# Another order of expert visits, and of weight widening beside it, in a fused attention, expert and feed-forward kernel

## The chip, the core and the metric

The kernel runs on one core of one Trainium2 chip. The metric is the device time of one launch in microseconds (us), the median of several executions; lower is better. Besides TensorE (PE), which multiplies matrices, the core has VectorE (DVE), ScalarE (ACT), GpSimd (POOL) and SyncE (SP). SP only issues transfers here. Every engine takes its instructions strictly in the order in which they were written, so an instruction that waits holds up all behind it on its engine.

## What is computed

Three stages follow each other: attention with rotary embedding over 4 batches, 8 heads and 576 positions (2304 tokens of width 512); a mixture of 8 experts, of which each token takes the best one; and a dense feed-forward with an ELU. Cut to what matters here:

```python
logits = xn @ en.T / tau
expert_idx = np.argmax(logits, axis=1)
for e in range(8):
    mask = expert_idx == e
    if not mask.any(): continue
    h = np.maximum(x[mask] @ w1[e], 0.0)               # w1[e]: 512 x 1024
    out[mask] = gate_w[mask, None] * (h @ w2[e])       # w2[e]: 1024 x 512
...
g = ELU(out @ w_in)                                    # w_in, w_out are float64
return g @ w_out
```

Which tokens go where is data. On the inputs of `setup_inputs()`, the reference sends 6, 709, 173, 0, 3, 691, 722 and 0 tokens to the experts 0 to 7. After the first three of the four batches it is 6, 706, 173, 0, 3, 118, 722 and 0.

## The kernel before, in words

Attention is worked pair of heads by pair of heads. As each batch ends, its tokens are routed: DVE counts how many tokens each expert has (`tot`), and GpSimd writes each token's row into the region of its expert in DRAM (`xreg`). Then the experts are worked in **visits** of 128 rows. One visit gathers 128 rows of one expert (`x_gather`, GpSimd), transposes them by a transfer (`x_turn`, SP), multiplies by w1 (`mm1`, four chunks of 24 matmuls, L1050 to L1052), applies `relu` (ACT, then DVE L1063), multiplies by w2 (`mm2`, 24 matmuls, L1087 to L1089), scales (`y_out`, ACT L1099 and DVE L1100) and writes 128 rows to `yreg` (`y_put`). TensorE runs mm1 of visit j+1 ahead of mm2 of visit j.

There are NE early visits, whose experts are chosen by `tab_early` from the counts after three batches (full tiles of 128 rows only, largest expert first), and NL late ones, whose experts are chosen by `tab_head` and `tab_visits` when all batches are counted. Before, NE is 6 and NL 19, so NV = 25 visits are written out. The last seven of them run only if they are needed (`used`), and what is not needed costs one tiny matmul each for mm1 and mm2. On the given inputs 22 are needed. `tab_head` ranks the experts by their visits still to do and then permutes the ranks by the table `pi` = 0, 7, 6, 5, 4, 3, 2, 1: the largest first, then from the smallest up. On the given inputs this order of visits follows, by the code's arithmetic:

- visits 0 to 4 expert 1, visit 5 expert 6 (early); visits 6 to 11 expert 5, 12 expert 4, 13 expert 1, 14 expert 0, 15 and 16 expert 2, 17 to 21 expert 6.

So the weights are loaded for the first visit and changed at visits 5, 6, 12, 13, 14, 15 and 17. A visit whose expert is that of the visit ahead skips loading and conversion by a branch on a register (`chg`, in `when`). A change costs, for one expert, eight loads of 512 KB on SP (`w_load(j, q)`, two each for q = 0 to 3, L1003 for w1 and L1006 for w2) and the split of each float32 chunk into two float16 halves (`w_conv(j, q)`: ACT L1023, then DVE L1025) into one set of buffers `w16`, so that a chunk is converted only when mm1 or mm2 of the visit ahead has used the old one.

Beside the visits, the float64 weights of the feed-forward are **widened**: 32 chunks of 512 KB, 0 to 15 of w_in and 16 to 31 of w_out, each with one `widen_load` (SP, L935 or L939) and five steps of `widen` (ACT L954, DVE L956 to L959, ACT L962 and for w_out four additions L965 to L968 on DVE or GpSimd, ACT L975, GpSimd L977). Chunks 11, 30 and 31 are widened much earlier and parked in DRAM.

**The order of all this is written out by due times.** Every task is put on a list by `add(t, f, ...)` or `addv(a, f, ...)`, the list is sorted by time, and the instructions of all engines are written in that order. In the expert part the unit (`ZU`) is half a visit: mm1 of visit j is due at 2j and mm2 at 2j + 3. `w_conv(j, q)` is due just after the visit ahead has used the chunks of q: at 2j - 1.74 and 2j - 1.24 for q = 0 and 1, at 2j + 1.26 and 2j + 1.76 for q = 2 and 3. `w_load(j, q)` is due as soon as one of 11 pairs of staging buffers is free, and the lists `wc` and `until` take a pair away for good when a widened chunk needs its room. Chunk c is widened at `WT[c]`, its load comes about 3 units earlier or when one of its few buffers is free, and the feed-forward begins at unit 50. There, g = 0 to 8 are groups of 256 rows gathered from `yreg` (`z_gather`, GpSimd; `z_turn`, SP), with `ff1`, `elu`, `ff2`, `fold` and `store`. The first two gathers are due at 37.7 and their transposes at 39.3.

Of the kernel before, what the change touches and what calls it, by code (L numbers as in the profile page):

```python
# [26 lines left out]
ROW = 520  # L27
NE = 6
NL = 19
NV = NE + NL  # L30
OFF = {'MX': 0.8, 'pool': (3, 8), 'pool13': (), 'pool14': (), 'pool15': (), 'rope0': (0, 1, 2, 4, 5), 'rope1': (0, 2), 'hi@1': -1.2, 'lo@1': -2.0, 'stack@1': -2.0, 'conv0': (5,), 'r_base': -0.39, 'r_norm': -0.46, 'r_slot@2': 0.6, 'r_gate': -0.41, 'r_put@0': 2.88, 'r_turn_pe@1': -3.85, 'r_sq@0': -0.13, 'r_rank@1': 0.52, 'r_rank': 0.35, 'r_turn:4': 0.24, 'relu@0': 2.65, 'r_acc_t@3': -0.16, 'r_pow@0': 1.01, 'r_sq@2': 0.29, 'r_base@2': -3.0, 'w_load@0': -0.15, 'x_turn@1': 1.47, 'r_put@1': 0.78, 'r_put:2': 0.5, 'w_load@1': -0.11, 'hi@2': -0.19, 'r_base@0': -0.49, 'r_pow@1': 0.4, 'r_slot:2': 0.04, 'rope2': (4,), 'r_gate@1': -0.33, 'r_gate@3': 0.36, 'r_slot@0': 2.38, 'x_gather@0': 0.7, 'hi': 0.06, 'r_norm@1': 0.22, 'r_acc_t@1': 0.35, 'v_load': 0.99, 'r_turn:0': 1.39, 'v_load@1:2': -0.43, 'r_pick': -0.18, 'r_rank@0': 0.21, 'r_turn': 1.14, 'r_pick@0': -0.28, 'WS': (14, 1.1, 32, 1.3), 'WO': (0, 0.476, 1.351, 1.395), 'WL': 3.126, 'WT': 8.011, 'relu': 0.901, 'y_out': -0.193, 'w_conv': 0.0, 'x_turn': 0.103, 'y_put': 0.0, 'G0': 51.007, 'ZG': -0.28, 'r_lo@1': 0.54, 'r_norm@0:0': -3.95, 'r_norm:0': -0.85, 'r_slot:4': -0.29, 'd_prep@3': -0.21, 'r_acc@13': 0.21, 'r_pick@1': -0.21, 'EO': (0, 0.3, 0.5, 0.7, 1.2), 'ES': (0, 1, 2, 3, 4, 5, 6, 7), 'WH': 0.32, 'WJ': 0.3, 'WE': 0.9, 'FO': (0.2, 0.25), 'E0': (1, 5, 6), 'EC': (0, 1, 2, 3, 4, 6, 7), 'WQ': (0, 1, 2, 3, 4, 8, 12, 14, 15), 'WR': (0, 1, 2, 3, 4, 5, 6, 7, 8, 9, 10, 11, 12, 13, 14, 15, 16, 17, 18, 19, 20, 21, 22, 23, 24, 25, 26, 27, 28, 29, 30, 31), 'c1': (1, 0), 'c2': (1, 0)}
# [13 lines left out]
def kernel(ctx: ExitStack, tc: tile.TileContext, qk, vp, cs, cf, tid, emb, tau, w1, w2, wi, wo, out, tag=None):  # L45
# [6 lines left out]
    yreg = dram.tile([NV * 128, ROW], I32, name="yreg")  # L52
# [578 lines left out]
    def tab_early():  # L631
# [42 lines left out]
        yield  # L674
        nc.vector.tensor_scalar(px, px, float(NE), None, op0=ALU.min)
# [5 lines left out]
        nc.vector.tensor_copy(sidx[:, 0:NE], cpos[:, 0:NE])  # L681
        yield

    def tab_head():
# [13 lines left out]
        nc.vector.scalar_tensor_tensor(key, nvi[:, 0], 8.0, e8, op0=ALU.mult, op1=ALU.subtract)  # L698
# [9 lines left out]
        nc.vector.tensor_tensor(m, rk.unsqueeze(2).to_broadcast([128, 8, 8]), e8.unsqueeze(1).to_broadcast([128, 8, 8]), op=ALU.is_equal)  # L708
        yield
        nc.vector.tensor_tensor(m, m, pi.unsqueeze(1).to_broadcast([128, 8, 8]), op=ALU.mult)  # L710
        yield
        nc.vector.tensor_reduce(out=rk, in_=m, op=ALU.add, axis=AX.X)
# [88 lines left out]
    for p in range(NP):  # L801
# [51 lines left out]
        if p % 4 == 3:  # L853
# [249 lines left out]
    def y_put(j):  # L1103
        nc.gpsimd.dma_start(out=yview[j][128 * j:128 * j + 128, :], in_=x2r.pop(j))
# [270 lines left out]
```

## Time and profile before

| | before |
|---|---|
| median of 3 executions | 1020.54 us (1019.59 to 1024.45) |
| the profiled execution: time, span of its instructions | 1029.22 us, 1027.4 us |
| PE busy | 902.9 us (88%), clock granted 0.95 |
| DVE busy | 694.3 us (68%) |
| ACT busy | 515.8 us (50%) |
| POOL busy | 560.8 us (55%) |
| read from memory | 87.54 MB |

The time is that of the launch, and the span goes from the first to the last instruction. Busy shares are averages over three stages with different limits: attention lasts to about 375 us, the visits from there to about 641, and the feed-forward from 645 to the end. A row of a timeline gives the start, the duration, engine, line, operation and, in brackets, how long the engine sat idle before it and what ended that.

### The profile page before, as it was taken

Reading aid. Unit: us, or ns where it says so; the run is one execution under the profiler, and the core shown is the slowest. Engines: PE = TensorE matmul, PEld = TensorE weight load, DVE = VectorE, ACT = ScalarE, POOL = GpSimd, SP = SyncE. Lnnn points to the kernel's source line nnn. Section 1 sums busy time; section 2 is a strip of 40 time slices with the busy share of each in tenths; the row PEclk is TensorE's granted clock in tenths of the full one; section 3 lists DMA queues with packets and bytes.
Section 4 is the critical chain, followed back from the end, with each engine's and each line's share of the span. In section 5 each row is a group of like instructions: output and inputs, shape, how many; then the busy total and the mean of one; then the engine's idle time right before and its main releaser. Section 6 shows DMA issues by size and latency. Waiting matters only on the chain. (4 is left out here: it accounts for less than half of the span.)

```text
span 1027.4 us, 24659 instructions
## 1 busy us (share of the span) xinstructions
PE 902.9 (88%) x9398; PEld 658.1 (64%) x9398; DVE 694.3 (68%) x1085; ACT 515.8 (50%) x874; POOL 560.8 (55%) x652
## 2 busy tenths in 40 slices
PE   3399998998889779999788995899899999999994
PEld 0144555545455467777555771688788888888884
DVE  8557668777866537888896766685665664665651
ACT  1244564464454624765675543565555554554540
POOL 6465765765634123434772165446776766766640
PEclk8589999999999889999999998899899999999998
DMA  7554565584364566998999873401201201201000
GB/s 257 158 154 113 153 163 129 170 173 115 122 147 165 167 183 142 317 229 228 277 320 284 237 181 90 119 14 42 62 22 43 59 25 43 58 27 42 22 22 20
DMA packets 133494, 136.04 MB, mean 132 GB/s; under 512 B 71528, under 2 KB 109416, under 8 KB 133360
## 3 DMA queue, kind: packets, MB, share of 16 engines
q1 hardware_dynamic: 124400, 106.07, 39.6%
q0 software_dynamic: 8352, 27.62, 8.2%
q8 instruction: 76, 1.25, 0.5%
q10 hardware_dynamic: 608, 0.63, 0.2%
q14 instruction: 58, 0.48, 0.2%
HBM read 87.54 MB, written 17.35 MB: 102 GB/s over the span
## 5 line engine op out<-in xcount | busy, mean ns | idle before, releaser
L1132 PE MATMUL banks<-arena 128*128 128x256 f16 x576 | 158.2, 275 | 2.8 <-ACT arena L1147 2.8
L1134 PE MATMUL banks<-arena 128*128 128x256 f16 x576 | 158.2, 275 | 0.0
L1133 PE MATMUL banks<-arena 128*128 128x256 f16 x576 | 158.2, 275 | 0.0
L364 ACT ACTIVATE arena<-banks 128x576 f32<-128x576 f32 x144 | 90.3, 652 | 124.2 <-PE banks L363 100.5
L1184 PE MATMUL banks<-arena 128*128 128x256 f16 x504 | 138.7, 275 | 5.5 <-DVE arena L1199 5.5
L1167 DVE TENSOR_TENSOR arena<-arena 128x896 f16<-128x896 f32 x72 | 80.2, 1114 | 87.1 <-ACT arena L1163 85.3
L1185 PE MATMUL banks<-arena 128*128 128x256 f16 x504 | 138.7, 275 | 0.0
L1186 PE MATMUL banks<-arena 128*128 128x256 f16 x504 | 138.7, 275 | 0.0
L1050 PE MATMUL banks<-arena 128*128 128x128 f16 x704 | 125.6, 224 | 7.2 <-ACT arena L1023 6.3
L1052 PE MATMUL banks<-arena 128*128 128x128 f16 x704 | 125.4, 225 | 4.7 <-DVE arena L1025 4.4
L1163 ACT ACTIVATE arena<-arena 128x896 f16<-128x896 f32 x71 | 67.5, 951 | 118.6 <-POOL arena L1160 117.3
L1051 PE MATMUL banks<-arena 128*128 128x128 f16 x704 | 125.5, 224 | 0.0
L336 DVE TENSOR_REDUCE MH<-banks 128x1 f16<-128x576 f32 x144 | 103.2, 751 | 31.6 <-PE banks L326 29.9
L1157 POOL TENSOR_TENSOR arena<-arena 128x256 f32<-128x256 f32 x67 | 53.1, 793 | 92.0 <-DVE arena L1154 90.5
L400 PE MATMUL banks<-arena 128*64 128x256 f32 (+9 forms) x768 | 90.2, 360 | 5.2 <-DVE arena L376 3.7
L1025 DVE SCALAR_TENSOR_TENSOR arena<-arena 128x1024 f16<-128x1024 f32 x64 | 82.3, 1324 | 17.2 <-ACT arena L1023 16.5
L977 POOL TENSOR_TENSOR arena<-arena 128x896 f16<-128x896 f32 (+1 forms) x32 | 52.6, 1645 | 69.4 <-ACT arena L975 50.3
L362 PE MATMUL banks<-arena 128*128 128x288 f16 (+1 forms) x320 | 79.6, 299 | 3.3 <-DVE l L522 2.0
L363 PE MATMUL banks<-arena 128*128 128x288 f16 (+1 forms) x320 | 78.7, 295 | 1.0 <-issue 1.0
L326 PE MATMUL banks<-arena 64*128 64x288 f16 (+1 forms) x320 | 47.6, 307 | 35.5 <-DVE MH L336 16.4
L1050 PEld LDWEIGHTS <-arena 128*128 128x128 f16 x704 | 70.9, 101 | 9.5 <-ACT arena L1023 6.9
L1087 PE MATMUL banks<-arena 128*128 128x512 f16 x176 | 67.5, 383 | 10.6 <-ACTq L987 10.1
(237 smaller groups left out, 2284.4 us busy)
## 6 DMA issues: line engine op xcount, KB each, us to landing
arena<-in_w_dram SPq DMA_DIRECT2D x64, 512.0 KB
arena<-in_qk_dram SPq DMA_DIRECT2D x30, 576.0 KB
arena<-in_wo_dram SPq DMA_DIRECT2D x32, 256.0 KB
arena<-in_wi_dram SPq DMA_DIRECT2D x16, 512.0 KB
arena<-arena SPq DMA_DIRECT2D x32, 216.0 KB
yreg<-arena POOLq DMA_DIRECT2D x25, 260.0 KB, 4.2
arena<-arena SPq DMA_DIRECT2D x32, 144.0 KB
arena<-in_vp_dram SPq DMA_DIRECT2D x16, 256.0 KB
```

What stands on the lines that cost most here:

```text
L336: nc.vector.tensor_reduce(out=MH1[p % 2][:, c:c + 1], in_=t[:, :, 0:288], op=ALU.max, axis=AX.XY, negate=True)
L364: nc.scalar.activation(P32[:, (9 * p + i) % RP].rearrange("p (c n) -> p c n", c=2), t[:, :, 0:288], AF.Exp, scale=2.0)
L400: nc.tensor.matmul(o[64 * e:64 * e + 64, c, 0:QC[c].stop - QC[c].start], lhsT=w, rhs=x[:, QC[c]], start=first and n == 0, stop=end and n = ...
L1050: nc.tensor.matmul(o[:, fc], lhsT=w[:, 0, a], rhs=x[:, k], start=k == 0, stop=False)
L1051: nc.tensor.matmul(o[:, fc], lhsT=w[:, 0, a], rhs=x[:, 4 + k], start=False, stop=False)
L1052: nc.tensor.matmul(o[:, fc], lhsT=w[:, 1, a], rhs=x[:, k], start=False, stop=k == 3)
L1132: nc.tensor.matmul(o[:, v], lhsT=wih[k][:, f0:f0 + 128], rhs=z[:, :, k], start=k == 0, stop=False)
L1133: nc.tensor.matmul(o[:, v], lhsT=wih[k][:, f0:f0 + 128], rhs=z[:, :, 4 + k], start=False, stop=False)
L1134: nc.tensor.matmul(o[:, v], lhsT=wil[k][:, f0:f0 + 128], rhs=z[:, :, k], start=False, stop=k == 3)
L1184: nc.tensor.matmul(y, lhsT=a, rhs=b, start=u + f + n == 0, stop=False)
L1185: nc.tensor.matmul(y, lhsT=a, rhs=w[:, 1, WB[i - 1]], start=False, stop=False)
L1186: nc.tensor.matmul(y, lhsT=q[:, 1, f, GB[i - 1]], rhs=b, start=False, stop=u + f == 4 and n == len(m) - 1)
```

## The change

Three things change. **The early visits** are five instead of six, and late ones 20 instead of 19. `yreg` gets `Y0` = 18432 unused rows in front, and the indices into it are raised by as much. **The order of the late visits**: the key by which `tab_head` ranks is raised by 512 for the expert of the last early visit, which so comes first, and the table `pi` gives way to arithmetic that subtracts 3.5 from the ranks 4 to 7: the order is rank 0, 4, 1, 5, 2, 6, 3, 7. On the given inputs, by the code's arithmetic:

- visits 0 to 4 expert 1 (early); visit 5 expert 1, 6 expert 0, 7 to 12 expert 5, 13 expert 4, 14 to 19 expert 6, 20 and 21 expert 2.

The weights are then changed at visits 6, 7, 13, 14 and 20, and 22 visits are needed as before. **The times** of the widening (`WT`), the first due time of loads for late visits (5.4 instead of 8.01) and of gathers (6 instead of 6.9, and no special time for visit 5) are other ones.

```diff
-NE = 6
-NL = 19
+NE = 5
+NL = 20
 NV = NE + NL
+Y0 = E * NTOK
...
-    yreg = dram.tile([NV * 128, ROW], I32, name="yreg")
+    yreg = dram.tile([Y0 + NV * 128, ROW], I32, name="yreg")
...
         nc.vector.tensor_copy(rrl, rr[:, 0, NE - 1:NE])
         yield
+        nc.vector.tensor_scalar(elast, e8, rrl, -512.0, op0=ALU.is_equal, op1=ALU.mult)
+        yield
+        nc.vector.tensor_tensor(elast, elast, e8, op=ALU.add)
+        yield
...
-        nc.vector.scalar_tensor_tensor(key, nvi[:, 0], 8.0, e8, op0=ALU.mult, op1=ALU.subtract)
+        nc.vector.scalar_tensor_tensor(key, nvi[:, 0], 8.0, elast, op0=ALU.mult, op1=ALU.subtract)
...
-        nc.vector.tensor_tensor(m, rk.unsqueeze(2).to_broadcast([128, 8, 8]), e8.unsqueeze(1).to_broadcast([128, 8, 8]), op=ALU.is_equal)
-        yield
-        nc.vector.tensor_tensor(m, m, pi.unsqueeze(1).to_broadcast([128, 8, 8]), op=ALU.mult)
-        yield
-        nc.vector.tensor_reduce(out=rk, in_=m, op=ALU.add, axis=AX.X)
+
+        ps_ = tbv(832, 8)
+        nc.vector.tensor_scalar(ps_, rk, 4.0, -3.5, op0=ALU.is_ge, op1=ALU.mult)
+        yield
+        nc.vector.tensor_tensor(rk, rk, ps_, op=ALU.add)
...
     def x_gather(j):
+        after('tab_early' if j < NE else 'tab_visits')
...
     def y_put(j):
-        nc.gpsimd.dma_start(out=yview[j][128 * j:128 * j + 128, :], in_=x2r.pop(j))
+        nc.gpsimd.dma_start(out=yview[j][Y0 + 128 * j:Y0 + 128 * j + 128, :], in_=x2r.pop(j))
...
-    WT = dict(zip((0, 1, 2, 3, 4, 5, 6, 7, 8, 9, 10, 12, 13, 14, 15), (4.6, 6, 6.65, 7.3, 8.6, 12.5, 14, 14.9, 15.7, 16.4, 17.1, 17.8, 18.5, 19.2, 19.9)))
-    WT |= dict(zip(range(16, 30), (20.8, 21.7, 22.9, 24.2, 25.2, 33.3, 35.3, 37.8, 38.6, 39.4, 40.2, 41, 41.8, 42.6)))
+    WT = dict(zip((0, 1, 2, 3, 4, 5, 6, 7, 8, 9, 10, 12, 13, 14, 15), (4.6, 6, 6.7, 7.4, 8.2, 9, 16, 16.85, 17.7, 18.55, 19.4, 20.25, 21.1, 21.95, 22.8)))
+    WT |= dict(zip(range(16, 30), (23.6, 30, 30.9, 31.8, 32.7, 33.6, 34.5, 35.4, 36.3, 37.2, 38, 39.3, 40.2, 42.2)))
...
-        if j < 6:
-            add(zg0 + 3.4 + .9 * j if j < 5 else max(zg4 + .1, ZV + ZU * 4.3 + .1), x_gather, j)
-        else:
-            addv(max(a - 5.2, 6.9), x_gather, j)
+        if j < NE:
+            add(zg0 + 3.4 + .9 * j, x_gather, j)
+        else:
+            addv(max(a - 5.2, 6), x_gather, j)
...
-        t0 = max(t0, free[b], {0: -4.8, 1: 0}.get(j, 1 if j < 6 else OFF.get('WT', 7.7))) + .001
+        t0 = max(t0, free[b], {0: -4.8, 1: 0}.get(j, 1 if j < NE else 5.4)) + .001
```

Left out are the three shifts of scratch room in `tab_visits` and `tab_compact`, the addition of `Y0` to `sidx` within instructions that were there, and the counts of `steps`, which follow the number of small operations: 24 instead of 22 in `tab_early`, 21 instead of 22 in `tab_head`.

## Rows read from the trace of the kernel before

**Rows 1.** Windows: us; then PE, PEld, DVE, ACT, POOL busy; granted clock; DMA share; GB/s

```profile
375.00:492.20 117.20, 117.20 (x1323) 85.94 (x1321) 97.59 (x164) 64.96 (x101) 48.69 (x62) 0.99 0.86 228
492.20:641.00 148.80, 120.34 (x1228) 83.53 (x1227) 112.55 (x145) 81.75 (x109) 76.70 (x83) 0.93 0.85 236
...
645.00:731.00 86.00, 79.56 (x671) 67.86 (x671) 59.85 (x91) 48.09 (x84) 49.61 (x73) 0.93 0.22 58
731.00:994.00 263.00, 262.55 (x2406) 235.08 (x2403) 157.97 (x211) 139.66 (x235) 175.26 (x255) 1.00 0.15 38
```

**Rows 2.** Timeline of PE: starts of mm1(2) and mm1(11), then around mm2(21)

```profile
386.70 0.22 PE L1050 MATMUL banks<-arena 128*128 128x128 f16 x1
...
481.56 0.22 PE L1050 MATMUL banks<-arena 128*128 128x128 f16 x1
...
622.51 0.60 PE L1076 MATMUL banks<-c,cft 1*128 1x512 f16 x2
633.24 0.58 PE L1087 MATMUL banks<-arena 128*128 128x512 f16 x1 [10.14 <-ACTq L987]
...
640.92 0.82 PE L1076 MATMUL banks<-c,cft 1*128 1x512 f16 x3
```

**Rows 3.** Who waited for whom, PE, 492 to 641 us: us, times, longest

```profile
PE banks L1087 <- ACTq L987: 10.1, 1, 10.1
PE banks L1050 <- ACT arena L1023: 6.3, 2, 3.2
PE banks L1052 <- DVE arena L1025: 4.4, 6, 1.7
PE banks L1088 <- DVE arena L1025: 4.1, 3, 2.2
```

**Rows 4.** Line L1003, w1's loads: durations ns, first and last start; L1006 likewise

```profile
L1003 SPq DMA_DIRECT2D arena<-in_w_dram x32: 72/390/1823, 324.9 to 558.9; - x32
```

**Rows 5.** Window: the stretch in which the transfers moved most

```profile
500.00:525.00 25.00, 18.02 (x143) 12.11 (x142) 22.38 (x23) 19.68 (x25) 18.89 (x20) 0.86 1.07 343
```

**Rows 6.** Groups by line, DVE, 375 to 660 us: count | busy us, mean ns | idle before

```profile
L1025 DVE SCALAR_TENSOR_TENSOR arena<-arena 128x1024 f16<-128x1024 f32 x56 | 72.0, 1324 | 12.6 <-ACT arena L1023 11.9 <-SPq L987 0.3 <-PE banks L1089 0.2
L1063 DVE SCALAR_TENSOR_TENSOR arena<-banks,arena 128x512 f16<-128x512 f32 x50 | 34.2, 685 | 17.2 <-ACT arena L1062 8.4 <-ACTq L987 4.1 <-DVEq L987 2.3
L958 DVE SCALAR_TENSOR_TENSOR arena<-arena 128x512 uint32<-128x512 uint32 x29 | 26.0, 897 | 4.8 <-POOL arena L977 2.3
L959 DVE SCALAR_TENSOR_TENSOR arena<-arena 128x512 uint32<-128x512 uint32 x29 | 23.3, 804 | 1.0
L956 DVE TENSOR_SCALAR arena<-arena 128x512 f32<-128x512 f32 x29 | 18.6, 643 | 5.4 <-DVEq L987 3.4
L1100 DVE SCALAR_TENSOR_TENSOR arena<-banks,arena 128x512 f16<-128x512 f32 x25 | 18.6, 746 | 14.6 <-ACT arena L1099 9.2 <-DVEq L987 3.6 <-ACTq L987 1.7
L957 DVE TENSOR_SCALAR arena<-arena 128x512 uint32<-128x512 uint32 x29 | 15.8, 546 | 1.0
```

**Rows 7.** Timeline of SP: loads of w1 for visit 17; load of chunk 28

```profile
555.66 5.05 SPq L1003 DMA_DIRECT2D arena<-in_w_dram  x4
...
618.27 1.46 SPq L939 DMA_DIRECT2D arena<-in_wo_dram  x2
```

**Rows 8.** Timeline of ACT: first conversion for visit 17; widening of chunk 28

```profile
563.33 1.06 ACT L1023 ACTIVATE arena<-arena 128x1024 f16<-128x1024 f32 x1 [5.34 <-DMA arena<-in_w_dram]
...
624.29 0.66 ACT L954 ACTIVATE arena<-arena 128x512 f32<-128x512 f32 x1 [5.39 <-DMA arena<-in_wo_dram]
```

**Rows 9.** What SP itself waited for, 370 to 660 us: us, times, longest

```profile
SPq L935 <- DVE arena L959: 26.3, 5, 20.7
```

**Rows 10.** Timeline of DVE, 611 to 615 us: two first steps of widening chunk 27

```profile
611.83 0.42 DVE L956 TENSOR_SCALAR arena<-arena 128x512 f32<-128x512 f32 x1
612.28 2.00 DVE L957 TENSOR_SCALAR arena<-arena 128x512 uint32<-128x512 uint32 x1
```

**Rows 11.** Timeline of POOL in the same stretch

```profile
612.01 2.00 POOL L977 TENSOR_TENSOR arena<-arena 128x896 f16<-128x896 f32 x1 [0.77 <-ACT arena L975]
```

More of the change, by code (lines that the diff above doesn't have):

```diff
@@ L680, in tab_early @@
         yield
-        nc.vector.tensor_copy(sidx[:, 0:NE], cpos[:, 0:NE])
+        nc.vector.tensor_scalar(sidx[:, 0:NE], cpos[:, 0:NE], float(Y0), None, op0=ALU.add)
         yield
@@ L734 @@
     rrl = const.tile([128, 1], F32, name="rrl")
+    elast = const.tile([128, 8], F32, name="elast")
     t1 = const.tile([128, 1], F32, name="t1")
@@ L744, in tab_visits @@
         yield
-        pr = tbv(2240, 3, n, 8)
+        pr = tbv(2304, 3, n, 8)
         nc.vector.tensor_tensor(pr, cm[:, 1:2].to_broadcast([128, 3, n, 8]), cof.unsqueeze(2).to_broadcast([128, 3, n, 8]), op=ALU.mult)
         yield
-        rr = tbv(4064, 3, n)
+        rr = tbv(4224, 3, n)
         nc.vector.tensor_reduce(out=rr, in_=pr, op=ALU.add, axis=AX.X)
@@ L764, in tab_compact @@
         n = NT - NE
-        cb = tbv(4300, 1, 8)
+        cb = tbv(0, 1, 8)
         nc.vector.scalar_tensor_tensor(cb[:, 0], nvi[:, 0], 128.0, nrest, op0=ALU.mult, op1=ALU.subtract)
         yield
-        cm = tbv(4336, n, 8)
+        cm = tbv(32, n, 8)
         nc.vector.tensor_tensor(cm, pre[:, 1:2].to_broadcast([128, n, 8]), cpos[:, 0:n].unsqueeze(2).to_broadcast([128, n, 8]), op=ALU.is_le)
@@ L772, in tab_compact @@
         yield
-        r = tbv(4720, n)
+        r = tbv(512, n)
         nc.vector.tensor_reduce(out=r, in_=cm, op=ALU.add, axis=AX.X)
         yield
-        nc.vector.tensor_tensor(sidx[:, NE:NT], r, cpos[:, NE:NT], op=ALU.add)
+        nc.vector.scalar_tensor_tensor(sidx[:, NE:NT], r, float(Y0), cpos[:, NE:NT], op0=ALU.add, op1=ALU.add)
         yield
@@ L877 @@
                 zt = q + dt * len(ops) + .1
-                steps(zt, .03, 22, tab_early)
+                steps(zt, .03, 24, tab_early)
                 zg0 = zt + 5 * sp
@@ L881 @@
                 zt = q + dt * len(ops) + .1
-                steps(zt, .12, 22, tab_head)
+                steps(zt, .12, 21, tab_head)
                 steps(zt + 2.7, .1, 10, tab_visits)
```

## The prediction

> **What bounds the kernel now.** I read the windows by stage first, then the timeline of TensorE in the expert part, then who waited for whom there, and last SP, ACT and DVE around the waits found.
>
> The windows show three kinds of stretch [rows 1]. From 375 to 492.2 us TensorE is busy for all of 117.2 us. From 492.2 to 641 it is busy for 120.3 of 148.8, at a granted clock of 0.93. In the feed-forward it is busy for 262.6 of 263 us from 731 on, so that part ends as much earlier as it starts earlier. Most of what an order of visits can win lies between 492 and 641.
>
> The unstalled pace comes from TensorE's timeline [rows 2]: mm1(2) starts at 386.70 and mm1(11) at 481.56, so a visit takes 94.86 / 9 = 10.54 us and a unit of the due times 5.27. At that pace mm2(20) would end at 481.56 + 11 x 10.54 = 597.5; the placeholder behind it starts at 622.51, so **25.0 us** are lost. mm2(21) takes about half a visit, 5.2 us (an estimate from the pace), yet it is over only at 640.92, which is 18.4 later: another **13.2 us**. Together 38.2.
>
> Who held it [rows 3]: 6.3 us for ACT's conversion (L1023), 4.4 and 4.1 for DVE's (L1025), and one wait of 10.1 on ACT ahead of mm2(21). With 3.6 us of smaller ones that is 28.5, and the other 9.7 are matmuls at the lower clock that follows the waits.
>
> Behind the first kind stand weights. w1 is loaded by 32 transfers and w2 by as many [rows 4], eight per expert: eight experts are loaded, and five of the changes fall on visits 12, 13, 14, 15 and 17. There the transfers run at 343 GB/s with a busy share of 1.07 [rows 5]. An expert is 4.19 MB, 12.2 us at that rate, and a visit lasts 10.54: changes in a row cannot be fed. Behind the second kind stands widening. ACT stood 5.39 us for the load of chunk 28 [rows 8], and relu(21), which mm2(21) needs, is queued behind it.
>
> **The change, part by part.**
>
> *Fewer changes.* Seven become five, so 16 loads (8.4 MB), 16 conversions on ACT and 16 of 1.324 us on DVE [rows 6], 21 us of DVE, go away. Off the path this is worth nothing by itself; its worth is in the waits.
>
> *Two pairs in a row instead of a chain.* Visits 6 and 7 change, then 13 and 14. The nearest rows are the changes at 5 and 6 of before: they lie in the stretch in which TensorE never idles [rows 1], with widening beside them. The loads have room as well. By the due times, loads for 6 and 7 lead their conversions by 4.5 units (24 us) and for 13 and 14 by 3 (15.8 us), against 2 to 2.5 for most of 13, 14 and 15 before; from the first load for 13 to the last conversion for 14 there are 8.5 units, 44.8 us, for 24.4 us of transfer. No chunk is due for widening between 24 and 30 now, so DVE has 16 x 1.324 + 3 visits of 2 x 0.685 + 0.746 = 2.1 [rows 6], 27.5 us of work in 31.6. I take 1 us lost, between 0 and 3.
>
> *The change at 20.* Loads q = 0 and 1 are due at 37.26 and 37.76, and mm1(20) at 40: 2.74 units, 14.4 us, from a staging room of two pairs. The nearest row is visit 17: issue at 555.66 [rows 7], first conversion at 563.33 after 5.34 us of waiting [rows 8], so 7.7 us to land beside other traffic. 7.7 + 1.06 for ACT + 4 x 1.324 for DVE = 14.1. It just fits, and each us by which SP comes late is paid. SP does come late when it stands for a widening buffer: 26.3 us in five waits [rows 9]. I take 3, between 0 and 8.
>
> *Widening at new times.* Twelve chunks (17 to 28) are due between 30 and 42 (63.2 us), beside the change at 20. DVE's four steps take 0.643 + 0.546 + 0.897 + 0.804 = 2.89 us a chunk [rows 6], so 34.7; the additions of six chunks, over 640 elements where the step of 512 takes 0.897, about 1.1 each (an estimate), 6.7; conversions 10.6; six visits 12.7: 64.7 in 63.2. DVE falls behind, by 1.5 us and by what it has to wait. Chunk 28 keeps its trap: its buffer comes free at 39.82, and it is due on ACT at 40.2, 2 us later, where its load took 6.0 us before, from 618.27 to 624.29 [rows 7, 8]. But then relu(20) and the conversions for mm2(20), not relu(21), are behind it, with 1 to 2 units of slack. On SP, loads q = 2 and 3 of visit 20 stand behind both z_turns and this widen_load; if SP is 8 us late they land about at 43, when mm2(20) is due. Against 13.2 lost here before I take 5, between 3 and 12.
>
> *Small ones.* `tab_early` gains two operations and `tab_head` loses one; none is on TensorE's path. They cost nothing, hidden behind matmuls; uncovered, three at 0.546, the shortest mean of these rows [rows 6], would be 1.6. The x_gather of visit 5 moves on GpSimd from 4.34 to 6, past small copies only, and its x_turn at 7.64 is 12 us ahead of its mm1 at 10. Loads for visit 6 are due at 5.76 behind the load of chunk 3, which waits for chunk 0's widening at 5.03; the tables are written by then, and the conversion is due at 10.26. `Y0` moves addresses only; no row shows such a move, and I take 0, between -1 and +1. The start at 375 and the feed-forward from 645 stay as they are. A clock not lowered by the 10.1 us wait may give up to 2.5 us at the start of the feed-forward (an estimate: half of 5.2); I count 0, since TensorE idles there for other engines anyway, busy for 79.6 of 86 us from 645 to 731 [rows 1].
>
> *Sum.* 38.2 lost before, 1 + 3 + 5 = 9 after: 29 us. Against the profiled execution, 1029.22 - 29 = 1000. The median of the runs is 8.7 below that execution. Some of the waits on transfers may be part of that difference, so I take 2 off: 27 us, 1020.5 - 27 = **993**. With the bounds, 3 to 23 lost after, 15 to 35 won, and 2 either way: 983 to 1007.
>
> *A rule against it.* DVE's second step took 2.00 us [rows 10] while GpSimd's subtraction ran from 612.01 to 614.01 [rows 11], and its mean is 0.546 [rows 6].
>
> The Trainium skill (SBUF — State Buffer, "Who interferes with whom") says that a DVE instruction in a two-port mode and a GpSimd one take the shared ports by an exclusive lock, and that the later one blocks until the other ends. The rows agree for this instance, and the rival "DVE becomes the bound" below is what it would make of the packed chunks.
>
> **Rivals.**
> - *Everything fits (12%).* All waits go, with the clock: 38 + 2 won, 981. For it: 117 us without a gap, with DVE at 97.6 of 117.2 [rows 1]. Against: the 2 us lead of chunk 28, which no slack in the order removes.
> - *DVE becomes the bound (15%).* If both short steps of the twelve chunks stood for GpSimd as in rows 10, each chunk would cost 2 x 2.00 - 0.643 - 0.546 = 2.8 more, 34 us; at half of that, 17, less 5 of slack, TensorE loses 12 more: 15 won, 1005. For it: the demand of 64.7 in 63.2. Against: the means hold such waits already, and the order of issue made few of them.
> - *SP is the new stop (5%, slower).* SP serves expert 2's loads, the widening loads and z_turn in one order. Were it held for 20.7 us, its longest wait [rows 9], once ahead of q = 0 and once ahead of q = 2, TensorE would lose 41 and the 13 of the end would stay: 54 - 38 = 16 slower, 1036. It decides from 12.5 us at each place, half of the 25 between 38 and 13. Against: that longest wait was one for a chunk that was not due yet, early in the part.
> - *It does not do what it says (4%).* If the waits of visits 12 to 17 came of widening on DVE and not of loads, as DVE's part of 8.5 us suggests [rows 3], the gain is the loads' 6.3, and the rest comes back at the packed stretch: 0 to 4 won, 1018.
>
> **How the numbers follow.** My forecast has 64%. Faster by over 0.5% (5 us, about what a measurement of this kernel can tell from no change): 64 + 12 + 15 = 91%; the same 4%; slower 5%. The range takes in the forecast's own and reaches into the two cases at its sides: 981 to 1007.
>
> **What would show it.** Right: 48 loads on L1003 and L1006 together instead of 64; TensorE without a gap up to mm1(13) and losing under 3 us up to mm1(15); lost time in the visits near 9 us, at mm1(20) and mm2(20); the feed-forward starting near 616 instead of 645 and as long as before. Wrong: waits on L1023 or L1025 of over 3 us at visits 6, 7, 13 or 14; a wait of 10 us ahead of mm2(20) or mm2(21); DVE over 95% busy between visits 15 and 20; a feed-forward longer by some us, if widening or its gathers come later than the visits' end.

## The result, and the profile after

The changed kernel takes 1009.04 us (median of 4 executions, 1006.17 to 1011.38), the one before beside it 1022.5 (median of 4): a ratio of 0.9874, 95% interval [0.9851, 0.9897]. (The two medians alone give 0.9868, well inside the interval.) The prediction had the direction right and twice the gain: 27 us forecast, 13.5 measured, 2 us above the upper end of the range.

The profiled execution takes 1010.61 us, its span 1008.8. Windows of the changed kernel, cut where visits 11, 14 and 18 begin on TensorE, at the feed-forward's first matmul (630.8) and as in [rows 1] behind it; the columns are those of [rows 1]:

```profile
385.70:480.60 94.90, 94.90 (x1082) 69.35 (x1081) 73.13 (x106) 55.30 (x81) 34.39 (x48) 1.00 0.86 235
480.60:512.20 31.60, 31.60 (x361) 23.11 (x360) 25.51 (x32) 22.04 (x30) 15.33 (x20) 1.00 1.14 291
512.20:554.40 42.20, 42.20 (x482) 30.84 (x481) 29.63 (x39) 23.57 (x33) 24.20 (x32) 1.00 0.78 218
554.40:630.80 76.40, 58.82 (x513) 35.27 (x511) 53.47 (x85) 34.73 (x50) 34.97 (x45) 0.87 0.58 161
630.80:714.00 83.20, 77.17 (x685) 67.42 (x685) 58.56 (x90) 46.73 (x82) 49.19 (x70) 0.98 0.22 57
714.00:975.00 261.00, 260.99 (x2391) 233.28 (x2389) 156.20 (x211) 139.00 (x234) 175.18 (x254) 1.00 0.15 38
```

From visit 2 to visit 17 TensorE now has no idle time at all, the two double changes (visits 6, 7 and 13, 14) included. Everything that is lost is lost in the fourth row, from the start of mm1(18) on: 17.6 us idle, and 58.8 us of matmuls that take 49.5 at the full clock (a run below shows that figure). In the kernel before the same cut gives these windows:

```profile
386.70:481.60 94.90, 94.90 (x1082) 69.39 (x1081) 82.82 (x125) 56.75 (x87) 38.10 (x48) 1.00 0.85 229
481.60:525.00 43.40, 34.92 (x362) 25.48 (x361) 39.23 (x44) 30.22 (x40) 31.28 (x35) 0.92 1.10 288
525.00:578.10 53.10, 45.44 (x481) 32.12 (x480) 40.35 (x45) 29.47 (x35) 17.66 (x21) 0.97 1.02 280
578.10:645.00 66.90, 52.40 (x513) 33.99 (x511) 44.77 (x77) 30.50 (x45) 35.39 (x40) 0.91 0.54 148
```

Against 94.9, 31.6, 42.2 and 49.5 us without loss, the kernel before lost 0, 11.8, 10.9 and 17.4, the changed one 0, 0, 0 and 26.9. So 22.7 us were won in visits 11 to 17 and 9.5 given back behind them. The visits begin 1.0 us earlier, and from the feed-forward's first matmul to the end it takes 378.0 us instead of 382.4. Together 13.2 + 1.0 + 4.4 = 18.6, the difference of the two profiled executions.

Who held TensorE in the fourth stretch (us, times, longest), and the longest of these waits in its timeline:

```profile
PE banks L1095 <- DVEq L993: 9.6, 3, 4.0
PE banks L1094 <- ACT arena L1069: 4.4, 1, 4.4
PE banks L1094 <- ACTq L993: 1.5, 2, 1.1
PE banks L1059 <- DVE arena L1031: 1.5, 2, 0.7
```

```profile
577.13 0.38 PE L1095 MATMUL banks<-arena 128*128 128x512 f16 x1 [2.65 <-DVEq L993]
591.09 0.58 PE L1095 MATMUL banks<-arena 128*128 128x512 f16 x1 [4.04 <-DVEq L993]
612.03 0.61 PE L1094 MATMUL banks<-arena 128*128 128x512 f16 x1 [4.43 <-ACT arena L1069]
621.51 0.59 PE L1095 MATMUL banks<-arena 128*128 128x512 f16 x1 [2.88 <-DVEq L993]
630.81 0.28 PE L1139 MATMUL banks<-arena 128*128 128x256 f16 x1
```

L1057 to L1059 are mm1 and L1094 to L1096 mm2 (L1050 to L1052 and L1087 to L1089 before), L1069 is ACT's relu, L1029 and L1031 are the conversion, and L993 is the branch of `when`. A wait "<-DVEq L993" means that DVE had not yet come to that place of its queue. It isn't one long stop, as the 10.1 us in [rows 3] were, but nine shorter ones: ACT and DVE are late again and again.

In part their timelines show why they are late. First DVE, ahead of and at visit 20's conversions (L962 to L965 are the first four steps of widening, L956 to L959 before):

```profile
559.34 1.90 DVE L962 TENSOR_SCALAR arena<-arena 128x512 f32<-128x512 f32 x1 [0.84 <-DVEq L993]
561.26 0.43 DVE L963 TENSOR_SCALAR arena<-arena 128x512 uint32<-128x512 uint32 x1
...
571.59 2.08 DVE L963 TENSOR_SCALAR arena<-arena 128x512 uint32<-128x512 uint32 x1
573.76 0.69 DVE L964 SCALAR_TENSOR_TENSOR arena<-arena 128x512 uint32<-128x512 uint32 x1
574.49 2.54 DVE L965 SCALAR_TENSOR_TENSOR arena<-arena 128x512 uint32<-128x512 uint32 x1
...
595.17 0.69 DVE L964 SCALAR_TENSOR_TENSOR arena<-arena 128x512 uint32<-128x512 uint32 x1
```

GpSimd in the same stretch (L983 is widening's last step, L977 before; L971 and L974 are additions):

```profile
559.02 1.88 POOL L983 TENSOR_TENSOR arena<-arena 128x896 f16<-128x896 f32 x1 [2.50 <-ACTq L993]
...
571.50 1.88 POOL L983 TENSOR_TENSOR arena<-arena 128x896 f16<-128x896 f32 x1 [2.50 <-ACTq L993]
...
574.52 0.73 POOL L971 TENSOR_TENSOR arena<-arena 128x256 f32<-128x256 f32 x1
...
576.02 0.44 POOL L974 TENSOR_TENSOR arena<-arena 128x128 f32<-128x128 f32 x1
...
595.40 2.21 POOL L983 TENSOR_TENSOR arena<-arena 128x896 f16<-128x896 f32 x1 [1.48 <-ACTq L993]
```

A widening step of DVE that begins while GpSimd's L983 runs ends only after it: 1.90 and 2.08 us for steps that otherwise take 0.43. A step that began beside GpSimd's four additions took 2.54 instead of 0.69. A step that began first kept its time: 0.69 us at 595.17, and there it was L983, begun at 595.40, that took 2.21 us instead of 1.88. These are [rows 10] and [rows 11] again, and here they come several times. ACT shows what follows (L960 and L981 are widening's first and fourth step):

```profile
572.89 0.66 ACT L960 ACTIVATE arena<-arena 128x512 f32<-128x512 f32 x1
576.21 1.06 ACT L1029 ACTIVATE arena<-arena 128x1024 f16<-128x1024 f32 x1 [2.66 <-DMA arena<-in_w_dram]
...
583.06 1.06 ACT L1029 ACTIVATE arena<-arena 128x1024 f16<-128x1024 f32 x1 [1.17 <-DMA arena<-in_w_dram]
584.02 0.94 ACT L981 ACTIVATE arena<-arena 128x896 f16<-128x896 f32 x1
```

From 573.6 to 584.0 ACT does nothing but stand for visit 20's loads and convert them, and the chunk that is half done (L981, 584.02) waits behind. SP had asked for those loads late (L1009 loads w1, L1012 w2; L1003 and L1006 before):

```profile
572.47 5.83 SPq L1009 DMA_DIRECT2D arena<-in_w_dram  x4
...
598.35 3.39 SPq L1012 DMA_DIRECT2D arena<-in_w_dram  x4
```

Ahead of the first of them, between 554.4 and 572.6 us, SP stood three times with a widening load (L945, L939 before) for a buffer that the last of DVE's four steps gives free (us, times, longest):

```profile
SPq L945 <- DVE arena L965: 7.6, 3, 2.8
```

So DVE's lag reaches visit 20's loads through SP's queue, in which these widening loads stand ahead of them.

### The profile page after: what moved, and what is told of

The parts are those of the page before. It is cut to its first block, busy times and chain, and to the rows that moved or that the text cites. A ratio compares the mean times of both kernels' runs of the same rounds, so it can differ in the third digit from the quotient of the medians.

```text
span 1008.8 us, 24500 instructions
## 1 busy us (share of the span) xinstructions
PE 901.2 (89%) x9398; PEld 655.4 (65%) x9398; DVE 669.7 (66%) x1070; ACT 502.3 (50%) x858; POOL 546.3 (54%) x652
## 5 line engine op out<-in xcount | busy, mean ns | idle before, releaser
L1059 PE MATMUL banks<-arena 128*128 128x128 f16 x704 | 122.4, 222 | 1.5 <-DVE arena L1031 1.5
L1057 PE MATMUL banks<-arena 128*128 128x128 f16 x704 | 122.5, 222 | 0.0
L1058 PE MATMUL banks<-arena 128*128 128x128 f16 x704 | 122.5, 222 | 0.0
L983 POOL TENSOR_TENSOR arena<-arena 128x896 f16<-128x896 f32 (+1 forms) x32 | 51.6, 1611 | 86.1 <-ACT arena L981 65.7
L1095 PE MATMUL banks<-arena 128*128 128x512 f16 x176 | 70.2, 399 | 10.2 <-DVEq L993 9.6
L1094 PE MATMUL banks<-arena 128*128 128x512 f16 x176 | 69.8, 396 | 6.0 <-ACT arena L1069 4.4
L377 POOL TENSOR_TENSOR arena<-arena 128x576 f16<-128x576 f32 x26 | 30.2, 1162 | 79.8 <-ACT arena L365 79.8
```

Of the source, the lines that this page charges most:

```text
L1057: nc.tensor.matmul(o[:, fc], lhsT=w[:, 0, a], rhs=x[:, k], start=k == 0, stop=False)
L1058: nc.tensor.matmul(o[:, fc], lhsT=w[:, 0, a], rhs=x[:, 4 + k], start=False, stop=False)
L1059: nc.tensor.matmul(o[:, fc], lhsT=w[:, 1, a], rhs=x[:, k], start=False, stop=k == 3)
```

## The experiments

One measure serves for all: the time from the start of mm1(18) to the feed-forward's first matmul (49.5 us without loss), and behind it the time to the first ff2 (31.0 in the changed kernel), both from TensorE's timeline. Ratios are to the kernel before on the same chip, with 95% intervals. The expectations name theories by letters (F is spelled out with e14), and put the loss of the changed kernel at 26 to 27.8 us; in this measure it is 26.9.

| kernel | lost in visits 2 to 10 | 11 to 13 | 14 to 17 | 18 to ff1 | ff1 to ff2, us | ratio |
|---|---|---|---|---|---|---|
| before | 0.0 | 11.8 | 10.9 | 17.4 | 34.0 | 1 |
| after | 0.0 | 0.0 | 0.0 | 26.9 | 31.0 | 0.9874 [0.9851, 0.9897] |
| e1 no widening of 17 to 29 | 2.2 | 0.0 | 0.0 | 0.0 | 30.4 | 0.9574 [0.9523, 0.9624] |
| e2 no change at 20 | 2.1 | 0.0 | 0.0 | 13.3 | 30.6 | 0.9751 [0.9697, 0.9806] |
| e16 no widening of 23 to 29 | 5.0 | 0.0 | 0.0 | 6.3 | 31.0 | 0.9660 [0.9613, 0.9708] |
| e14 two chunks behind the visits | 1.2 | 0.0 | 0.0 | 21.5 | 39.5 | 0.9873 [0.9843, 0.9903] |
| e15 four chunks behind the visits | 0.9 | 0.0 | 0.0 | 12.7 | 53.8 | 0.9950 [0.9921, 0.9979] |
| e6 ACT instead of GpSimd | 0.0 | 0.0 | 0.0 | 22.8 | 30.7 | 0.9818 [0.9772, 0.9864] |
| e4 third buffer | 6.1 | 0.0 | 0.0 | 28.4 | 30.7 | 0.9865 [0.9820, 0.9911] |
| e5 other order in a chunk | 2.0 | 0.0 | 0.0 | 28.0 | 30.8 | 0.9873 [0.9802, 0.9945] |
| e12 one more slot | 1.0 | 0.0 | 0.0 | 26.0 | 30.3 | 0.9843 [0.9805, 0.9880] |
| e7 new order, old times | 5.5 | 9.6 | 3.9 | 23.1 | 33.1 | 1.0045 [1.0021, 1.0070] |
| e9 old order, new times | 0.0 | 1.4 | 18.3 | 19.9 | 31.0 | 0.9990 [0.9970, 1.0010] |
| e8 three more in attention | 0.0 | 0.0 | 0.0 | 17.5 | 31.3 | 0.9919 [0.9895, 0.9943] |
| e10 three moved, wider apart | 1.2 | 3.5 | 1.3 | 17.6 | 31.7 | 0.9847 [0.9824, 0.9870] |
| e11 the same, other places | 0.0 | 0.0 | 5.7 | 21.3 | 31.3 | 0.9899 [0.9883, 0.9914] |
| e13 mixed | 4.4 | 2.3 | 0.8 | 24.9 | 31.1 | 0.9882 [0.9856, 0.9908] |

Up to visit 10, e1, e2, e4, e5, e12, e14, e15 and e16 hold the same instructions as the changed kernel, and yet their profiled executions lose 0.9 to 6.1 us there, with one wait of TensorE for transposed rows in each, and its own none. That is how much single executions differ, and why the columns of the later visits say more than small differences of ratios.

### What the loss hangs on: widening, the change at 20, or both

e1 leaves out the widening of chunks 17 to 29 (GpSimd clears their room):

```diff
     def widen_load(w, c):
+        if w == 1 and 1 <= c <= 13:
+            return
...
     def widen(w, c, i):
+        if w == 1 and 1 <= c <= 13:
+            if i == 0:
+                nc.gpsimd.memset(wos[c // 2][:, 0, :, c % 2], 0.0)
+                nc.gpsimd.memset(wos[c // 2][:, 1, :, c % 2], 0.0)
+            return
```

> The changed kernel without the widening of chunks 17 to 29: their loads and five steps are left out, GpSimd clears their room instead, so the feed-forward multiplies zeros there. Theory A (widening runs at about 6.2 us a chunk against 4.74 due, and its lag makes SP, the loads for visit 20 and the relus late): loads for visit 20 are issued near 561 instead of 572, the visits lose 0 to 5 us instead of 27.8, and mm2(21) ends near 604. Theory B (the change at 20 itself, with its short lead and two pairs of staging, is the cause): the visits still lose 12 us or more, and mm2(21) ends after 614.

Its fourth stretch has no idle time:

```profile
557.20:606.70 49.50, 49.50 (x514) 33.60 (x512) 20.49 (x24) 18.38 (x25) 18.48 (x33) 1.00 0.76 179
```

and SP asks for visit 20's loads (L1016 and L1019 there) 7.6 and 23.6 us after the start of mm1(18) at 557.22, where the changed kernel did so after 18.1 and 44.0:

```profile
564.84 3.67 SPq L1016 DMA_DIRECT2D arena<-in_w_dram  x4
...
580.77 3.44 SPq L1019 DMA_DIRECT2D arena<-in_w_dram  x4
```

So the change at 20 costs nothing by itself, as theory A expected. e2 keeps the widening and leaves out the loads and conversions of visit 20, which works with the old weights:

```diff
     def w_load(j, q, n):
+        if j == 20:
+            return
...
     def w_conv(j, q, n):
+        if j == 20:
+            return
```

> The changed kernel without loads and conversions for visit 20: visits 20 and 21 multiply by the weights of the visit ahead. Theory A: widening lags as before, chunk 26 by about 8 us, and relus queued behind it still cost 6 to 14 us of the 27.8. Theory B: the visits lose under 4 us, and mm2(21) ends near 605.

```profile
559.20:622.00 62.80, 53.06 (x513) 34.29 (x511) 44.51 (x78) 27.17 (x43) 35.53 (x45) 0.95 0.49 132
```

13.3 us are lost by widening alone, in the range of theory A, and 26.9 by both; half of the loss belongs to neither by itself. The change at 20 is free without the widening of these chunks, and costs 13.6 us beside it.

### Lag brought along, one stop, or a price for each chunk

e16 is e1 with `7 <= c <= 13` in place of `1 <= c <= 13`, so it leaves out chunks 23 to 29 alone.

> Chunks 23 to 29 are not widened (GpSimd clears their room), 17 to 22 are, at the changed kernel's times. Theory F: the visits before have no loss, as in the changed kernel, and the stretch from visit 18 on loses what the lag of the chunks before leaves: 49.5 to 53 us, ratio 0.958 to 0.964. Rival (chunks 17 to 22, 4.7 us apart, build up the lag that is paid at visit 20): 56 to 65 us, ratio 0.966 to 0.976.

The stretch takes 55.8 us, between the two expectations and nearer the rival's. 6.3 us are lost, which is what chunks 17 to 22 leave behind, with the change at 20 in its place; in visits 14 to 17, beside which they are due, they cost nothing. So about a quarter of the loss is lag brought along. The other 20.6 us come with the seven chunks, 2.9 each on average. e14 and e15 move two and four of them behind the visits:

```diff
-    WT |= dict(zip(range(16, 30), (23.6, 30, 30.9, 31.8, 32.7, 33.6, 34.5, 35.4, 36.3, 37.2, 38, 39.3, 40.2, 42.2)))
+    WT |= dict(zip(range(16, 30), (23.6, 30, 30.9, 31.8, 32.7, 33.6, 34.5, 35.4, 36.3, 37.2, 38, 39.3, 45.6, 46.8)))   # e14
+    WT |= dict(zip(range(16, 30), (23.6, 30, 30.9, 31.8, 32.7, 33.6, 34.5, 35.4, 36.3, 37.2, 44.6, 45.8, 47, 48.2)))   # e15
```

> Chunks 28 and 29 go from 40.2 and 42.2 units to 45.6 and 46.8, behind the matmuls of visit 20 and in front of the first group of the feed-forward (which reads these weights 30 us after its start). From visit 18 on TensorE needs 49.5 us without any widening, 76.4 in the changed kernel with seven chunks. Theory F (each chunk in these last visits costs them about 4 us, whatever its place among the others): 68 to 70 us there, 0 to 3 us more in the first group, ratio to the kernel before 0.979 to 0.984. Rival (it is one stop at visit 20 that costs, not the number of chunks): 74 to 77 us there, ratio 0.986 to 0.99.

> Chunks 26 to 29 behind the visits (44.6, 45.8, 47.0 and 48.2 units). Theory F: 58 to 64 us from visit 18 on; the first group of the feed-forward waits 0 to 10 us more for its ELU steps, which stand in the same queues behind them: ratio 0.973 to 0.984. Rival (the one stop at visit 20): 72 to 77 us from visit 18 on, ratio 0.986 to 0.995.

The visits take 71.0 and 62.2 us: they win 5.4 us by two chunks and 14.2 by four, 2.7 and 3.6 for each. e15 lies in the range of theory F; e14's 71.0 lies between the two ranges, 1 us above F's and 3 below the rival's. Together they show a price for each chunk, somewhat below F's 4 us, and not one stop. But both ratios missed F, because the first feed-forward group pays 8.5 and 22.8 us for the chunks, where 0 to 3 and 0 to 10 were expected. In e15 TensorE waits there once for 20 us, on ACT's ELU steps, which stand behind the chunks in the queue (us, times, longest, from 610 to 690):

```profile
PE banks L1139 <- ACT arena L1154: 21.9, 3, 20.2
```

Work that is put off isn't hidden by that. These weights are read only 31 us later, but what is read at once waits behind them.

### What makes a chunk slow

e6 makes the low half of chunks 17 to 29 by a copy on ACT in place of the subtraction on GpSimd, so these low halves lack the difference:

```diff
                 nc.scalar.activation(h, x, AF.Copy)
+            elif 17 <= 16 * w + c <= 29:
+                nc.scalar.activation(l, x, AF.Copy)
+                wad.pop((w, c))
             else:
```

> For chunks 17 to 29 the subtraction that makes the low half of a widened piece is a copy on ScalarE in place of a subtraction on GpSimd (their low halves are wrong so). Theory C (a chunk of w_out is a chain over three engines in order, in which GpSimd's 1.9 us subtraction stops VectorE's next steps): the period of a chunk falls from about 6.2 us to 4.7 to 5.2, the visits lose about 10 us less than the 26 of the changed kernel, ratio to the kernel before 0.975 to 0.98. Rival (VectorE's and ScalarE's sum of work sets the period): the period stays near 6, ScalarE has 1 us more per chunk, ratio 0.985 to 0.995.

DVE's steps now have their short times in the same stretch (L996 is L993 of the changed kernel):

```profile
557.59 0.43 DVE L962 TENSOR_SCALAR arena<-arena 128x512 f32<-128x512 f32 x1 [0.84 <-DVEq L996]
558.05 0.43 DVE L963 TENSOR_SCALAR arena<-arena 128x512 uint32<-128x512 uint32 x1
558.57 0.69 DVE L964 SCALAR_TENSOR_TENSOR arena<-arena 128x512 uint32<-128x512 uint32 x1
559.30 0.69 DVE L965 SCALAR_TENSOR_TENSOR arena<-arena 128x512 uint32<-128x512 uint32 x1
```

2.24 us for the four, where their means in the changed kernel's fourth stretch are 0.848, 0.637, 0.695 and 1.121, together 3.30. The Trainium skill (SBUF — State Buffer, "Who interferes with whom") has the rule that GpSimd shares a pair of ports with DVE, and that of two instructions that need it whoever comes second stands until the other is done. e6 agrees, since the long steps go with GpSimd's subtraction. But the loss falls by 4.1 us and not by 10, and the time between the starts of two chunks (21 to 26) from 6.1 to 5.7 us and not to about 5. The 4.1 us are a net figure: the copies make ACT busier (41.18 us in this stretch against 34.73), so what GpSimd costs alone isn't shown. And they rest on one execution of each kernel, since the intervals of the two ratios overlap. GpSimd's part is real; taking it away in this manner won little.

Three other edits did nothing that can be told from the changed kernel. e4 gives the chunks from 22 on a third pair of work buffers (the ring in the expectation is the chain of a chunk's steps, closed by the wait for one of two such pairs; the first use of the third list overwrites a chunk that is still at work, whose values are lost):

```diff
+    wat3 = Turns([at("PL", U32, 512, add=4096 + 2048 * i) for i in range(2)] + [at("sq", U32, 512)])
+    wdt3 = Turns([at("PL", U32, 7, 128, add=8192 + 3584 * i) for i in range(3)])
...
-            wad[w, c] = (ea, ed) if 16 * w + c in EARLY else (wat(), wdt())
+            wad[w, c] = (ea, ed) if 16 * w + c in EARLY else (wat3(), wdt3()) if 16 * w + c >= 22 else (wat(), wdt())
```

> The changed kernel with a third pair of scratch buffers for the widening of chunks 22 to 29. Theory A, if its ring is closed by the two buffers: chunks follow each other every 4.7 us, chunk 27 lags under 4 us instead of 20, the visits lose about 10 us, and the time is 988 to 998. Theory B: unchanged, 1005 to 1012. A third theory (DVE and GpSimd block each other at the shared ports, whatever the buffers): lag and time as without it.

e5 writes the third step of a w_out chunk a little earlier:

```diff
-            addv(t + WO[i] * d, widen, c // 16, c % 16, i)
+            addv(t + (WO[i] - .1 * (c >= 16 and i == 2)) * d, widen, c // 16, c % 16, i)
```

> The changed kernel with one number changed: step 2 of the widening of w_out is due 0.11 units earlier, so that DVE takes the additions of a chunk ahead of the first steps of the next one and not behind them. Theory A: the ring of six links over two buffers shrinks to 4.4 to 5 us a chunk, chunk 27 lags under 6 us, and the time is 990 to 1000. Theory B and that of the ports: unchanged, 1005 to 1012.

e12 lets chunks 24 and 25, which end the use of a staging slot, change places with 26 and 27:

```diff
+    WT |= dict(zip(range(16, 30), (23.6, 30, 30.9, 31.8, 32.7, 33.6, 34.5, 35.4, 38.3, 39.3, 36.3, 37.2, 40.2, 42.2)))
```

> Chunks 24 and 25 change places with 26 and 27 (24 and 25 at 38.3 and 39.3 units, 26 and 27 at 36.3 and 37.2). 24 and 25 are written where a staging slot for the experts' weights lies, so that slot stays in use for two units more, and the first quarter for visit 20 is asked for at 36.02 in place of 37.26 units. Theory E (the load for visit 20 has to wait until ScalarE and VectorE have passed the conversions of visit 18 in their queues, because only two slots are left, and that makes the lag of the widening a stop of TensorE): visits lose 4 to 10 us less than the changed kernel's 26, ratio to the kernel before 0.978 to 0.984. Rival (the amount of work in the queues alone sets the loss): as the changed kernel, 0.985 to 0.99.

28.4, 28.0 and 26.0 us lost against 26.9. In e12 the first load for visit 20 did come earlier, 13.3 us after the start of mm1(18) instead of 18.1, and the second quarter 2.5 earlier (20.3 against 22.9), but w2's half did not (44.4 against 44.0). The ratio lies between the two expectations, but by the trace theory E falls: one slot more moves the first loads, and the loss stays within 1 us.

### The order and the times, each alone

e7 is the changed kernel with the old `WT`, e9 the kernel before with the new one. The second of its two lines, as e7 changes it:

```diff
...
-    WT |= dict(zip(range(16, 30), (23.6, 30, 30.9, 31.8, 32.7, 33.6, 34.5, 35.4, 36.3, 37.2, 38, 39.3, 40.2, 42.2)))
+    WT |= dict(zip(range(16, 30), (20.8, 21.7, 22.9, 24.2, 25.2, 33.3, 35.3, 37.8, 38.6, 39.4, 40.2, 41, 41.8, 42.6)))
```

> The new order of visits with the widening times of the kernel before. Theory C: the last seven chunks stand 4.2 us apart, under the period of about 6 that a chunk of w_out takes, so the lag is as large as with the new times: visits lose 20 to 32 us, ratio 0.982 to 0.993. Rival (the new times themselves do the harm, the order alone would bring the forecast gain): visits lose under 15, ratio 0.97 to 0.977.

> The kernel before with the new widening times alone (order of visits as before). Theory C: chunks 17 to 26 come 4.74 us apart and lag in the same way, while the old order's stops at its four early changes of expert stay: about as before, ratio 0.992 to 1.008. Rival (the times bring the whole gain of the change, the order nothing): ratio 0.985 to 0.99.

Neither wins anything: the order (with the rest of the change) is 0.45% slower, the times alone make no difference. With the old times chunks 6 to 20 stand between units 14 and 25.2, and the new order loads for visits 13 and 14 from about unit 21 and converts from 24.3 on: 13.5 us are lost in visits 11 to 17, and 23.1 behind them. With the old order the new times move the loss from visits 11 to 13 (11.8 to 1.4) into visits 14 to 17 (10.9 to 18.3), where experts still change while chunks 17 to 21 come close together. Only both together put the changes at 6, 7, 13 and 14 where no chunk is due; that this is why they lose nothing is read from the due times. e7 missed both expectations, since it loses ahead of the last visits too; e9 came as theory C expected.

### Another place for the chunks

e8 widens 27 to 29 early, in attention, and spaces the others wider; e10 moves 26, 27 and 17 into gaps ahead of unit 30; e11 puts those three beside the changes of 13 and 14; e13 combines e10's two early chunks with a third slot.

```diff
-    EARLY = {30: 12, 31: 13, 11: 14}
+    EARLY = {27: 9, 28: 10, 29: 11, 30: 12, 31: 13, 11: 14}   # e8
...
+    WT |= dict(zip(range(16, 30), (23.6, 30, 31.05, 32.1, 33.15, 34.2, 35.25, 36.3, 37.35, 38.4, 39.45, 42.4, 44.5, 44.6)))   # e8
+    WT |= dict(zip(range(16, 30), (23.6, 24.6, 29.9, 31, 32.1, 33.2, 34.3, 35.4, 36.5, 39.2, 12.4, 14.2, 40.4, 42.2)))   # e10
+    WT |= dict(zip(range(16, 30), (23.6, 24.5, 29.9, 31, 32.1, 33.2, 34.3, 35.4, 36.5, 39.2, 25.6, 27.4, 40.4, 42.2)))   # e11
+    WT |= dict(zip(range(16, 30), (23.6, 30, 31, 32, 33, 34, 35, 36, 39.2, 40.3, 12.4, 14.2, 41.3, 42.4)))   # e13
```

> Chunks 27, 28 and 29 of the first widened set are widened early, in attention, and kept; chunks 17 to 26 stand 1.05 units (about 5.5 us) apart in place of 0.9 (4.74). Theory C: the chain of a chunk keeps up, the lag of the last chunks stays under 6 us, the visits lose under 8 us in place of 26, and attention pays 0 to 6 us for three more chunks: ratio 0.965 to 0.975. Rival (attention has no room: the three chunks cost there what they save): ratio 0.98 to 0.99.

> Three of the chunks that the changed kernel widens from 30 units on are moved into the stretches where it widens none (26 and 27 to 12.4 and 14.2, 17 to 24.6); those that are left, 18 to 24, stand 1.1 units (5.8 us) apart, and none stands at the change of expert of visit 20 (25 at 39.2, 28 at 40.4, 29 at 42.2). Theory D (a chunk of w_out takes some 6 us from start to start however it is ordered, and a late chunk holds the conversions of visit 20, which wait for their load in the same queues and hold the next chunks in their turn): visits lose 3 to 10 us in place of 26, ratio to the kernel before 0.965 to 0.977. Rival (the engines have no room for these chunks anywhere, as the attempt to widen three in attention suggests): the early visits lose what the late ones win, ratio 0.983 to 0.993.

> As the run before, but all three moved chunks stand between 24.5 and 27.4 units, where the two changes of expert of visits 13 and 14 are. Theory D: these conversions and the three chunks get in each other's way in the same queues, as at visit 20: visits lose 6 to 14 us, ratio 0.968 to 0.981. Rival (there is room beside these changes): as the run before, within 0.3%.

> Two chunks early (26 at 12.4, 27 at 14.2 units), 17 to 23 from 30 on with 1.0 unit (5.3 us) between them, 24, 25, 28 and 29 after the change of visit 20 (39.2, 40.3, 41.3, 42.4), so that the third slot stays in use until then. Theory E with D (lag and missing slot together): visits lose 8 to 14 us, ratio 0.970 to 0.980. Rival (the stretch from 36 units on stays the bound because the four last chunks and the second half of visit 20 fall together): 0.983 to 0.988, with the loss after the last change.

e8 wins 9.4 us in the last visits, and attention pays for it: mm1(2) starts at 397.9 us instead of 385.7, 12.2 later for three chunks. e10 wins 9.3 there and loses 6.0 in the visits ahead. e11 wins 5.6 and loses 5.7 ahead, half a per cent behind e10; theory D had the sign of that difference, the rival (within 0.3%) had not. e13 wins 2.0 and loses 7.5. The theories' ratios were all missed. In e10 the rival's range held (no room); in e8 and e13 the ratio lies just above the rival's range, but the losses stand where the rival had them (e8 in attention; in e13 18.8 of the 24.9 us come after the start of mm1(21)). Spacing the chunks 5.5 to 6 us apart did not bring the loss from visit 18 on under 10. e10 (0.9847) and e12 (0.9843) have the lowest ratios of the kernels that do all the work, but their intervals overlap with the changed kernel's, so no faster version was found. In each place a chunk costs about what it saves elsewhere.

## Why the prediction was right and wrong, step by step

- **What bounds the kernel.** The amount is right: it put the loss of the visits at 38.2 us, and the four stretches give 40.1. The cause that it gave for the larger part, weights of changes in a row that cannot be fed, is not borne out as the whole: e9 keeps all seven changes, moves only the widening, and loses 1.4 us in visits 11 to 13 instead of 11.8. There too changes and widening cost by lying side by side.
- **Fewer changes, two pairs in a row.** Right, and the largest part of the gain. w1 and w2 are loaded by 24 transfers each, as forecast 48, and visits 6, 7, 13 and 14 lose nothing where 1 was taken. What the prediction didn't say is that this needs the new times: e7 has the same changes and loses 13.5 us in visits 11 to 17.
- **The change at 20.** The step that failed, with the next. It was priced at 3 us, between 0 and 8, as a term of its own, and added. By itself it costs 0 (e1). Beside the widening it costs 13.6 (26.9 against 13.3 in e2). The sum had noted that each us by which SP comes late is paid, and that SP comes late when it stands for a widening buffer. That is what happened, at another size: SP was late by 10.5 us ahead of q = 0 and by 20.4 ahead of q = 2 (18.1 and 44.0 against 7.6 and 23.6 in e1). 7.6 of the 10.5 are waits for widening buffers, and of the 20.4 a wait of 4.8 for a staging slot stands right ahead of the load. No run gave the widening loads another buffer or put visit 20's loads ahead of them, so what SP's lateness is worth by itself stays open.
- **Widening at new times.** The term that was mis-sized: 5 us, bounds 3 to 12; measured 13.3 without the change at 20, and with it 6.3 brought along from chunks 17 to 22 and 20.6 from the seven others. The demand was about right: 64.7 us of DVE's work in 63.2 was forecast, and in the fourth stretch DVE does 53.5 us of work where TensorE needs 49.5. Some 8 of these 53.5 are DVE standing for GpSimd (an estimate: eight chunks at 3.30 us instead of 2.24). The forecast put DVE behind by 1.5 us "and by what it has to wait", without a number for the waiting, and so took its time as usable to the last us. DVE is busy for 70% of that stretch (53.47 of 76.40), 71% in e2, 67% in the kernel before (44.77 of 66.90) and 63% in e10. At the 67% of before, which stood in its trace, 53.5 us of work would take 80; 76.4 were measured. That is an argument from likeness, and no run shows the share to be a limit: in visits 2 to 10 of before DVE is busy for 87% (82.82 of 94.90) and nothing is lost, beside chunks that are mostly of w_in, which have no additions.
- **Chunk 28's trap.** It didn't come as such: no wait of TensorE is longer than 4.43 us. In its place are nine of 0.5 to 4.4.
- **The feed-forward.** The clock was counted as 0 with up to 2.5 us to win. The feed-forward is 4.4 us shorter, 3.0 of them up to the first ff2: 31.0 us at a granted clock of 1.00, instead of 34.0 at 0.92, with TensorE busy for 29.6 and 32.2.
- **Profile and median.** 2 us were taken off. The profiled executions differ by 18.6 us, the medians by 13.5, so 5 was right: the profiled execution of before stands 6.7 us above the median beside it, that of after 1.6. So 13.2 in the visits, 1.0 ahead of them and 4.4 behind, less 5.1, make the 13.5; the forecast had 29 in the visits, less 2. That the miss was no larger is in part luck, since the 1.0 and 4.4 were counted as 0.
- **Rivals.** "DVE becomes the bound" (1005) came nearest in time and partly in cause: the steps stretched by GpSimd are there, but taking them away won 4 us net (e6), not 12. "SP is the new stop" had the two places right (ahead of q = 0 and q = 2) and in part the reason, waits of the widening loads; they were three of 2 to 3 us ahead of q = 0 and not one of 20.7. "Everything fits" is out. So is the time of "it does not do what it says", but what it said of visits 12 to 17, that their waits come of widening, is borne out for visits 11 to 13 by e9.

The signs named in advance pointed the right way: no gap up to mm1(15), and a feed-forward that starts at 630.8 rather than near 616. DVE "over 95% busy" between visits 15 and 20 as a sign of trouble was the wrong sign: the trouble came with 70% from visit 18 on.

Why engines that are busy for 70% lose 27 us is shown only in part. That each chunk in the last visits costs about 3 us, and that widening beside it makes the change at 20 dear, is shown by e1, e2 and e14 to e16. Of the chain itself (ACT, DVE, ACT, DVE or GpSimd, ACT, GpSimd, each in its own fixed order) only a copy on ACT in place of GpSimd's subtraction was tried, and which link holds the others stays open. A version with the same work in another order on each engine was not tried beyond e5.

## What to carry to other kernels

When a plan fills an engine of several that hand work to each other in a fixed order, compare the demand also with the share that this engine has reached in a like stretch (here 0.63 to 0.71), not only with 1; this is a rule of thumb from these traces, which no run tested. Two edits that use the same queues don't add: here a change of weights cost 0 alone and 14 us beside the widening, so price them together, or leave a gap between them as the two double changes have. And work moved out of a crowded stretch has to be priced where it goes: two chunks won 5.4 us in the visits and cost 8.5 behind them.

## What the runs showed of the hardware

A skipped branch still orders. Visits 18 and 21 need no conversion, and yet two of SP's loads for visit 20 wait until DVE has come past a branch of `when`. By the code's due times these branches are skipped conversions of visit 18 (ahead of q = 1, L1009) and visit 21 (ahead of q = 2, L1012), which have the staging slot right before (us, times, longest, SP from 520 to 631 in the changed kernel):

```profile
SPq L1012 <- DVEq L993: 4.8, 1, 4.8
SPq L1009 <- DVEq L993: 2.5, 1, 2.5
```

Short waits cost clock as well: of the 26.9 us lost in the fourth stretch 17.6 are idle time, in nine pieces of 0.5 to 4.4 us, and 9.3 are matmuls at a lower granted clock (0.87 over the stretch). That is half as much again as the pieces last. In e2 9.7 us of idle time came with 3.6 of slower matmuls, at 0.95.
